# A build-time list scheduler for the order of all engine work, smaller last gating groups, 16 output slots and an input ring of 16, in a scan with a mixture of adapters

## The chip, the cores and the metric

The kernel runs on one core of one Trainium2 chip. The metric is the device time of one execution in microseconds (us), of which the profiler's span (first to last instruction) is about 1.8 us less. Times are medians of several executions. "ns" is written where nanoseconds are meant. PE is the matrix engine (TensorE), DVE is VectorE, ACT is ScalarE, POOL is GpSimd, SP is the engine whose queue issues the loads and stores.

## The reference, cut to what matters

A linear recurrence over 8 sequences of 6400 steps with 128 channels, then a top-2-of-8 mixture of rank-16 adapters on each of the 51200 rows, added to the row.

```python
def _attn_ref(a, b):                      # a, b: (8, 6400, 128) float32
    for t in range(S):
        h = a[:, t] * h + b[:, t]
        out[:, t] = h
def _moe_ref(x, w_gate, A, B):            # x = out as (51200, 128)
    logits = x @ w_gate                   # 8 experts
    topk = np.argpartition(-logits, K, axis=1)[:, :K]      # K = 2
    ... w = softmax of the two chosen logits ...
    delta[mask] += w[mask, k, None] * (x[mask] @ A[e]) @ B[e]
    return (x + delta).astype(np.float32)
```

## The kernel before

The rows are cut into 100 units of 512. For each unit w, PE transposes a and b into PSUM, the on-chip memory for its results (`pA`, `pB`), ACT copies `pA` to SBUF, the on-chip memory for everything else (`a_st`), DVE scans along time into `xT`. PE then makes the logits (`pL`) and x·A (`pZ`); once per group of 4 units the gates are made: an ACT copy, a DVE reduction, three POOL instructions, a second reduction, four POOL instructions, and a sigmoid on ACT. DVE multiplies `pZ` by the gates (`zw`), PE transposes the product (`pT`), ACT copies it (`zwT`), PE adds zwT·B and x in `pO`, ACT copies that to an output buffer (`outt`), and SP stores it.

In this program every engine runs a fixed list of instructions in order; semaphores make it wait for others. The list comes from a loop over steps written by hand:

```python
RING, XR, G, OU, NOUT = 24, 16, 4, 2, 4   # input units, x units, group, units per store, output buffers
LAG = G + 4
for s in range(-1, NU + LAG + 3):
    v = s - LAG
    if ok(v):      z_mm(v)                                  # PE
    if ok(s + 1):  transposes("A", s + 1); a_evac(s + 1)    # PE, ACT
    if ok(v - 1):  zw_tr(v - 1); t_evac(v - 1)              # PE, ACT
    if ok(s + 1):  transposes("B", s + 1)                   # PE
    if ok(v - 2):  delta(v - 2); o_evac(v - 2); ...store of a pair...
    if ok(s - 1):  logits(s - 1); ...l_evac at a group's end...
    if ok(s):      scan(s)                                  # DVE
    c = s - G - 1
    if c >= 0 and c % G == 0 and c // G < NU // G:
        gate_m1(c // G); gate1(c // G)                      # DVE, POOL
    c = s - G - 2
    if c >= 0 and c % G == 0 and c // G < NU // G:
        gate_m2(c // G); gate2(c // G)                      # DVE, POOL
        gate_sig(c // G)                                    # ACT: the sigmoid, in this same step
    if ok(v):      z_mul(v)                                 # DVE
    ...next load, when its ring slot comes free...
```

(Reformatted to one line per branch, cuts marked by dots.) There is one `pA`, one `pT`, one `pO`, two `pB`, two `pZ` and one `pL`, eight PSUM buffers in all.

## Time and profile before

| | before |
|---|---|
| time, median of 3 | 245.56 us |
| span of the profiled run | 243.7 us |
| first scan, last scan start | 6.6 us, 221.1 us |
| middle: period of 4 units | 8.46 us |
| from the start of the last scan to the end | 22.6 us |

No engine is full on average. From the page of before, the busy time of each engine, then two rows of its 40 slices of 6.1 us (each digit is the busy share in tenths):

```profile
PE 208.9 (86%) x2800; PEld 195.4 (80%) x2800; DVE 193.4 (79%) x257; ACT 172.5 (71%) x352; POOL 87.9 (36%) x181
...
DVE  0755988946889888988998898889889888987430
...
DMA  7999999999999999999999999999998233422444
```

DVE holds 8 or 9 tenths in the middle but falls at the start, near 50 us (the 4) and at the end, while DMA is busy until about 180 us and then at 2 to 4 tenths. So the kernel is read stage by stage.

**The middle.** The timeline of before on DVE in one period; columns are start, duration, instruction, and in brackets the idle time before it and what ended it:

```profile
91.53 0.68 DVE L412 TENSOR_TENSOR zw<-pZ,g 128x512 f16<-128x512 f32 x1
92.12 1.27 DVE L267 TENSOR_TENSOR_SCAN xT<-a_st,xT,pB 128x512 f16<-128x512 f32 x1
93.41 0.28 DVE L347 TENSOR_REDUCE m_0<-L_0 128x16 f32<-128x128 f32 x1
...
95.39 0.67 DVE L412 TENSOR_TENSOR zw<-pZ,g 128x512 f16<-128x512 f32 x1
96.84 1.28 DVE L267 TENSOR_TENSOR_SCAN xT<-a_st,xT,pB 128x512 f16<-128x512 f32 x1 [0.78 <-ACT a_st L249]
```

DVE starts one instruction right behind the other (a scan every 1.19 us, a multiply 0.59) until it waits 0.78 us for the `a_st` copy. The timeline of before on ACT at that time says why the copy was late:

```profile
94.08 0.59 ACT L454 COPY outt<-pO 128x512 f32<-128x512 f32 x1
96.02 0.31 ACT L390 ACTIVATE g<-um 128x128 f32<-128x128 f32 x1 [1.36 <-POOL um L379]
96.24 0.57 ACT L249 COPY a_st<-pA 128x512 f32<-128x512 f32 x1
```

ACT stands 1.36 us at the sigmoid, waiting for POOL; the copy behind it needs nothing from the sigmoid. This recurs in each group.

**The whole run.** The groups of waits of before (waiting instruction, what released it: us in total, times, longest):

```profile
ACT g L390 <- POOL um L379: 34.8, 24, 2.6
DVE xT L267 <- ACT a_st L249: 21.2, 23, 2.8
...
ACT outt L454 <- DMA out_dram<-outt: 6.0, 2, 3.5
```

The last line is the hole near 50 us: ACT waits twice, 3.5 and 2.5 us, for one of the 4 output buffers.

### The profile page before, as it was taken

The page shows a single profiled execution, that of the slowest core. Times are in us where ns is not written, and L with a number is a line of the kernel's source. Part 1 is how long each engine was busy: PE and PEld are TensorE (multiplying, and loading weights), DVE is VectorE, ACT ScalarE, POOL GpSimd, SP SyncE. Part 2 cuts the span into 40 slices and gives each one's busy share as a digit, 9 for nine tenths or more (in the row PEclk, how much of TensorE's full clock was granted, in tenths as well). Part 3 has the DMA queues.
Part 4 walks back from the last instruction along what each step waited for, and adds up shares of the span by engine and source line. Part 5 has one row for each costly group of instructions (what it writes and reads, how often), then busy time and mean ns, then how long its engine had stood idle before and what let it go on. Part 6 is the DMA issues. An engine that isn't in the chain of part 4 may idle for free.

```text
span 243.7 us, 6924 instructions
## 1 busy us (share of the span) xinstructions
PE 208.9 (86%) x2800; PEld 195.4 (80%) x2800; DVE 193.4 (79%) x257; ACT 172.5 (71%) x352; POOL 87.9 (36%) x181
## 2 busy tenths in 40 slices
PE   3766989867899999999999999999999999997592
PEld 2666888867889888988998898889889888986471
DVE  0755988946889888988998898889889888987430
ACT  3223587556777977887797788779777977977572
POOL 1005424503245235424522542353255235324500
PEclk9989999979999999999999999999999999999978
DMA  7999999999999999999999999999998233422444
GB/s 200 387 387 389 383 387 386 387 392 396 402 396 399 392 400 401 395 400 396 400 395 391 360 386 386 343 405 350 342 404 330 104 134 128 156 108 105 156 175 172
DMA packets 41424, 79.23 MB, mean 325 GB/s; under 512 B 2864, under 2 KB 2992, under 8 KB 41392
## 3 DMA queue, kind: packets, MB, share of 16 engines
q1 hardware_dynamic: 40064, 78.65, 86.7%
q8 instruction: 22, 0.36, 0.6%
q10 hardware_dynamic: 1328, 0.14, 0.4%
q14 instruction: 10, 0.08, 0.1%
HBM read 52.56 MB, written 26.21 MB: 323 GB/s over the span
## 4 chain that ended last, share of the span: by engine, by line
PE 32%; POOL 21%; DVE 20%; DMA 10%; ACT 8%; issue 6%; SPq 1%; POOLq 0%; DVEq 0%; ACTq 0%
DVE xT L267 12%; PE pA L237 10%; PE pB L237 8%; POOL pn L365 6%; DMA out_dram<-outt 5%; ACT a_st L249 5%; PE pT L421 5%; DVE zw L412 5%; DMA b_in<-in_b_dram 4%; POOL um L379 4%; PE pO L440 3%; PE pO L443 3%; PE pZ L398 2%; POOL d_0 L372 2%; POOL d_1 L372 2%
## 5 line engine op out<-in xcount | busy, mean ns | idle before, releaser
L267 DVE TENSOR_TENSOR_SCAN xT<-a_st,xT,pB 128x512 f16<-128x512 f32 x96 | 120.2, 1252 | 26.8 <-ACT a_st L249 21.2
L237 PE MATMUL pA<-ident_f,a_in 128*128 128x128 f32 x400 | 64.7, 286 | 18.5 <-ACT a_st L249 13.6
L249 ACT COPY a_st<-pA 128x512 f32<-128x512 f32 x100 | 58.8, 588 | 19.4 <-PE pA L237 18.4
L412 DVE TENSOR_TENSOR zw<-pZ,g 128x512 f16<-128x512 f32 x100 | 67.4, 675 | 5.1 <-PE pZ L398 3.2
L454 ACT COPY outt<-pO 128x512 f32<-128x512 f32 x100 | 58.9, 589 | 9.9 <-DMA out_dram<-outt 6.0
L237 PE MATMUL pB<-ident_f,b_in 128*128 128x128 f32 x400 | 62.8, 281 | 2.3 <-DMA b_in<-in_b_dram 2.3
L237 PEld LDWEIGHTS pA<-ident_f,a_in 128*128 128x128 f32 x400 | 43.8, 145 | 22.9 <-ACT a_st L249 16.8
L440 PE MATMUL pO<-cst_h,zwT 128*128 128x128 f16 x400 | 56.6, 222 | 5.6 <-ACT outt L454 5.5
L431 ACT COPY zwT<-pT 128x512 f16<-128x512 f16 x100 | 59.6, 596 | 1.0 <-PE pT L421 0.8
L443 PE MATMUL pO<-ident_h,xT 128*128 128x128 f16 x400 | 56.6, 222 | 0.0
L237 PEld LDWEIGHTS pB<-ident_f,b_in 128*128 128x128 f32 x400 | 44.0, 145 | 3.4 <-DMA b_in<-in_b_dram 3.2
L443 PEld LDWEIGHTS pO<-ident_h,xT 128*128 128x128 f16 x400 | 45.2, 115 | 1.0
L440 PEld LDWEIGHTS pO<-cst_h,zwT 128*128 128x128 f16 x400 | 39.4, 99 | 7.4 <-ACT outt L454 7.3
L421 PE MATMUL pT<-ident_h,zw 128*128 128x128 f16 x400 | 39.3, 222 | 4.3 <-ACT zwT L431 2.7
L398 PE MATMUL pZ<-cst_h,xT 128*128 128x128 f16 x400 | 39.7, 222 | 0.0
L421 PEld LDWEIGHTS pT<-ident_h,zw 128*128 128x128 f16 x400 | 28.8, 99 | 9.2 <-DVE zw L412 3.7
L390 ACT ACTIVATE g<-um 128x128 f32<-128x128 f32 x25 | 7.8, 311 | 34.8 <-POOL um L379 34.8
L323 POOL TENSOR_TENSOR d_0<-Lg,m_0 128x128 f32<-128x128 f32 x13 | 5.3, 408 | 71.5 <-DVE m_0 L312 71.5
L289 PE MATMUL pL<-cst_h,xT 128*128 128x8 f16 x400 | 27.1, 173 | 0.0
L398 PEld LDWEIGHTS pZ<-cst_h,xT 128*128 128x128 f16 x400 | 27.0, 116 | 0.0
L289 PEld LDWEIGHTS pL<-cst_h,xT 128*128 128x128 f16 x400 | 24.4, 116 | 0.1
L323 POOL TENSOR_TENSOR d_1<-Lg,m_1 128x128 f32<-128x128 f32 x12 | 4.9, 407 | 49.8 <-DVE m_1 L312 49.8
(29 smaller groups left out, 107.9 us busy)
## 6 DMA issues: line engine op xcount, KB each, us to landing
out_dram<-outt SPq DMA_DIRECT2D x50, 512.0 KB, 7.8
a_in<-in_a_dram SPq DMA_DIRECT2D x24, 1024.0 KB, 10.6
b_in<-in_b_dram SPq DMA_DIRECT2D x24, 1024.0 KB, 12.7
a_in<-in_a_dram SPq DMA_DIRECT2D x2, 256.0 KB, 3.6
b_in<-in_b_dram SPq DMA_DIRECT2D x2, 256.0 KB, 4.1
a_in<-in_a_dram SPq DMA_DIRECT2D x1, 512.0 KB, 5.5
b_in<-in_b_dram SPq DMA_DIRECT2D x1, 512.0 KB, 6.4
cst_f<-in_moe_A_dram ACTq DMA_DIRECT2D x1, 64.0 KB, 4.1
```

The source lines that it names most:

```text
L237: last = h.transpose(view[:, i, :], ring[:, w % RING, i * 128 : (i + 1) * 128], ident_f[:, :],)
L249: lambda h: h.copy(a_st[w % 2][:, :], pA[:, :]),
L267: last = h.tensor_tensor_scan(out=xT[:, x0 + lo : x0 + hi], data0=a_st[w % 2][:, lo:hi], data1=pB[w % 2][:, lo:hi], initial=init, op0=ALU. ...
L289: last = h.matmul(pL[:, c : c + E], x_block(w, i), wg_h)
L365: lambda h: h.tensor_scalar(pn[s][:, :, :], d2[s][:, :, :], 0.0, -1.0e30, ALU.is_lt, ALU.mult),
L398: last = h.matmul(pZ[w % 2][:, i * 128 : (i + 1) * 128], x_block(w, i), Acat_h)
L412: lambda h: h.tensor_tensor(out=oview, in0=zview, in1=gview, op=ALU.mult),
L421: last = h.transpose(pT[:, i * 128 : (i + 1) * 128], zw[w % 2][:, i, :], ident_h[:, :])
L431: lambda h: h.copy(zwT[w % 2][:, :], pT[:, 0:UT]),
L440: h.matmul(o, zwT[w % 2][:, i * 128 : (i + 1) * 128], Bcat_h, start=True, stop=False)
L443: last = h.matmul(o, x_block(w, i), ident_h[:, :], start=False, stop=True)
L454: lambda h: h.copy(outt[j % NOUT][:, w % OU, :], pO[:, :]),
```

## The change

The hand-written loop goes. Each instruction group gets a name, an engine, a priority key (its unit number plus an offset), an assumed duration and its dependencies; a list scheduler simulates the five engines and a 390 GB/s DMA link at build time and picks, on each engine as it falls free, the ready item with the lowest key. The result is again one fixed order for each engine. Beside that: gating groups of 4 end in groups of 2, 1, 1; loads are 1, 1 and then 2 units (before 1, 1, 2, then 4); 16 output slots instead of 4 pairs, the last two units stored singly; the input ring is 16 units instead of 24. The diff, cut to its core (assumed durations in ns):

```diff
+    def schedule(self, dma_rate):
+        ...
+            pick = min((x for x in cand[e] if x[0] <= t), key=lambda x: (x[1].key, x[0]))
+            self.order[e].append(op)
+            free[e] = t + op.busy
-    RING = 24
+    RING = 16
-    NOUT = 4
+    NOUT = 16
+    loads = cut((1, 1), 2, ())
+    groups = cut((), 4, (2, 1, 1))
+    stores = cut((), 2, (1, 1))
+            add(f"{kind}{w}", "pe", w - (0.3 if kind == "A" else 0), 440.0, ...)
+                f"scan{w}", "dve", w, 1140.0, emit, ...
+            add(f"Z{w}", "pe", w + 5, 230.0, emit, [f"scan{w}", f"mul{w - NZ}", "cst"])
+                f"mul{w}", "dve", w + 5.5, 600.0, ...
+            add(f"T{w}", "pe", w + 6, 225.0, emit, [f"mul{w}", f"tev{w - 1}", "idh"])
+                f"tev{w}", "act", w + 6, 480.0, ...      # needs T{w}, R{w - 2}
+            add(f"R{w}", "pe", w + 6.5, 455.0, emit, [f"tev{w}", f"oev{w - NO}"])
+                f"oev{w}", "act", w + 6.5, 480.0, ...    # needs R{w}, the slot's store
-        for s in range(-1, NU + LAG + 3):
-            ... the whole loop by hand ...
+        plan.schedule(390.0)
```

(Lines of several calls are joined here.) In what follows T is the transpose of the product into `pT`, "tev" its copy to `zwT`, R the output matmuls into `pO`, "oev" their copy to `outt`, as the change names them.

## The prediction

> **What bounds it now.** The span is 243.7 us (the time is about 1.9 us longer). No engine is full on average (page, part 1: PE 86%, DVE 79%, ACT 71%), so I read stages.
>
> - Middle (59 to 222 us). The chain of waits repeats every 8.46 us per 4 units (2.116 per unit). In one period (DVE timeline, 88.3 to 96.8 us) VectorE works back to back except for one gap of 0.78 us, charged to the a_st copy. That copy is late because ScalarE is stuck for 1.36 us at the sigmoid, which waits for POOL. The Trainium skill ("TensorE: Matmul & The Clock Gate", section "Architectural detail") calls ACT and DVE strict FIFO; the trace agrees: a copy that needs nothing from the sigmoid waits behind it. Outside that gap VectorE needs 7.68 us per 4 units (scan 1.19 start to start, multiply 0.59, reductions 0.19 each), 1.92 per unit; PE is also back to back there, 1.91 per unit.
> - Start (6.6 to 59 us). Only 23 scans. VectorE waits for pB behind 1 MB loads (2.7 us once); ScalarE waits twice for an output buffer (3.5 and 2.5 us, "ACT outt <- DMA"): only 4 store pairs exist, and stores queue behind loads (one took 13 us).
> - End. 22.6 us from the start of the last scan: fixed lag of 8 units, a full group's gating exposed, 512 KB last store.
> - DMA is busy until about 180 us, then 35 to 50%. It moves 78.65 MB; its best stretches show 397 to 402 GB/s, so about 198 us: near, but not binding in the middle.
>
> **What the change does.** Instruction kinds, sizes and bytes stay (a few small gating instructions are added). Order moves: (1) in the built program the sigmoid stands two units after the second reduction, about 3.8 us, while POOL's four instructions need about 2.0 us; the 0.78 us gap should go: 0.17 to 0.19 per unit. (2) Loads of 512 KB: first ten scans end near 20 us, not 25. (3) 16 output slots: the two output waits go, about 6 us of VectorE idle. (4) Last groups of 2, 1, 1, lag down to 5 to 6, single-unit last stores: tail about 16 us, saving 6.
>
> **Sum (an estimate from the durations above).** Ten scans by 20 us. Left for VectorE: 90 x 1.19 + 100 x 0.585 + 48 x 0.19 = 175 us; at 97% packed, 180: ends at 200. Exposed last gating 2 us, then transpose, copy, PE, copy, store of the last unit about 7 (7.6 in before): span 209 to 212. Nearly all of it is on the critical path, but PE (191 us plus a slow start), VectorE and DMA all end near 205 to 210, so a static order cannot make every stall vanish; I add 2 us. The shorter ring should not hurt: 16 units are 31 us, far over the 8 to 13 us from issue to landing.
>
> **Predicted: 214 us, 8 in 10 between 208 and 223.** Faster by over 2%: 0.97; within: 0.02; slower: 0.01.
>
> **What would show it.** Middle period 7.7 to 7.9 us per 4 units, DVE busy about 97%; "DVE xT <- ACT a_st" from 21 us to under 6; "ACT g <- POOL um" (34.8 us) below 8; "ACT outt <- DMA out_dram" gone; DMA busy to nearly the end, mean near 370 GB/s; tail about 16 us; instruction durations unchanged.
>
> **What would make it wrong.** DMA binding: below 385 GB/s with mixed traffic, waits on a_in/b_in would appear mid-run. The order was made with assumed durations (scan 1.14 against 1.19); if it mismatches, PE or ScalarE waits appear every unit and the period stays above 8 us. SP may hold loads behind an unready store. A lower granted clock would stretch everything.

## The result, and the profile after

222.91 us (222.17 to 223.05, 4 runs) against 245.55 us (4 runs): the ratio is 0.907, 95% interval 0.905 to 0.909. Ratios are computed as the mean time of one kernel's runs over that of the other's of the same rounds, so they are not quite the ratios of the medians quoted. The change saved 22.6 us; the prediction had said 214 us with a range of 208 to 223, so the result lies at the very edge of it.

| | before | after |
|---|---|---|
| span of the profiled run | 243.7 | 221.2 us |
| last scan starts | 221.1 | 197.35 us |
| middle: period of 4 units | 8.46 | 7.81 us |
| last scan start to end | 22.6 | 23.9 us |

The page after:

```profile
PE 204.4 (92%) x2800; PEld 195.6 (88%) x2800; DVE 191.5 (87%) x261; ACT 174.2 (79%) x356; POOL 90.5 (41%) x195
...
DVE  0499999999999999999999999999999999994320
...
DMA  7999999999999999999999999999999999843434
```

The holes at the start and near 50 us are gone; DVE is full until about 199 us, DMA until about 188. The chain that ended last is now PE's, 82% of the span (before, 32%). The waits after:

```profile
ACT outt L505 <- PE pO L494: 27.5, 76, 1.1
...
DVE zw L465 <- ACT g L442: 5.1, 21, 0.5
...
ACT g L442 <- POOL um L433: 0.5, 2, 0.3
```

The sigmoid waits 0.5 us instead of 34.8, and no wait of `outt` for a store is listed. In the timeline of after on DVE one period of the middle runs from one small gap to the next, 106.81 to 114.62, 7.81 us:

```profile
106.81 0.69 DVE L465 TENSOR_TENSOR zw<-pZ,g 128x512 f16<-128x512 f32 x1 [0.30 <-ACT g L442]
107.42 0.28 DVE L369 TENSOR_REDUCE m_0<-Lg 128x16 f32<-128x128 f32 x1
...
113.11 1.27 DVE L313 TENSOR_TENSOR_SCAN xT<-a_st,xT,pB 128x512 f16<-128x512 f32 x1
114.62 0.69 DVE L465 TENSOR_TENSOR zw<-pZ,g 128x512 f16<-128x512 f32 x1 [0.23 <-ACT g L442]
```

What did not shrink is the tail: 23.9 us from the start of the last scan, 1.3 us more than before. Nine multiplies and eleven sets of output matmuls are left when the last scan starts or soon after, and they go at 1.8 to 1.9 us each (the last one 2.2), although no engine is busy for much over half of the time there. The window of after from 200 us (us: busy time with instructions of PE, PEld, DVE, ACT, POOL, then granted clock, DMA share and GB/s):

```profile
200.00:221.00 21.00, 10.94 (x144) 9.01 (x144) 6.12 (x13) 11.20 (x26) 5.61 (x20) 0.82 0.40 151
```

The timelines of after in the tail, PE first:

```profile
207.26 0.41 PE L449 MATMUL pZ<-cst_h,xT 128*128 128x128 f16 x4 [0.79 <-DVE zw L465]
207.51 0.22 PE L493 MATMUL pO<-cst_h,zwT 128*128 128x128 f16 x1
...
207.95 0.39 PE L472 MATMUL pT<-ident_h,zw 128*128 128x128 f16 x4
209.13 0.41 PE L449 MATMUL pZ<-cst_h,xT 128*128 128x128 f16 x4 [0.79 <-DVE zw L465]
209.38 0.22 PE L493 MATMUL pO<-cst_h,zwT 128*128 128x128 f16 x1
```

then ACT, and last DVE:

```profile
206.77 0.59 ACT L483 COPY zwT<-pT 128x512 f16<-128x512 f16 x1
...
208.15 0.59 ACT L505 COPY outt<-pO 128x512 f32<-128x512 f32 x1 [0.67 <-PE pO L494]
208.64 0.59 ACT L483 COPY zwT<-pT 128x512 f16<-128x512 f16 x1
210.03 0.59 ACT L505 COPY outt<-pO 128x512 f32<-128x512 f32 x1 [0.80 <-PE pO L494]
```

```profile
206.51 0.69 DVE L465 TENSOR_TENSOR zw<-pZ,g 128x512 f16<-128x512 f32 x1 [1.18 <-PE pT L472]
...
208.38 0.69 DVE L465 TENSOR_TENSOR zw<-pZ,g 128x512 f16<-128x512 f32 x1 [1.09 <-PE pT L472]
```

Two loops can be followed there. R of one unit (207.51) lets the output copy start (208.15); the `zwT` copy of the next unit stands behind that copy on ACT (208.64 to 209.23), and the next R needs it (209.38): 1.87 us. Likewise on PE: a transpose that needs only an older product and the `zwT` copy of 206.77 to 207.36 stands in PE's order behind a Z that waits for the newest multiply (207.26) and behind R, and so starts at 207.95; the next multiply waits for it. The Trainium skill ("TensorE: Matmul & The Clock Gate", Part 2, step-by-step) says that matmuls stay in program order and only weight loads are pulled ahead; the trace agrees, the order of PE's matmuls is that of the list.

### The profile page after: what moved, and what is told of

It reads as the page before. It is cut to its first block, busy times and chain, and to the rows that moved or that the text cites. A ratio compares the mean times of both kernels' runs of the same rounds, so it can differ in the third digit from the quotient of the medians.

```text
span 221.2 us, 6969 instructions
## 1 busy us (share of the span) xinstructions
PE 204.4 (92%) x2800; PEld 195.6 (88%) x2800; DVE 191.5 (87%) x261; ACT 174.2 (79%) x356; POOL 90.5 (41%) x195
## 3 DMA queue, kind: packets, MB, share of 16 engines
q1 hardware_dynamic: 40848, 78.65, 94.3%
## 4 chain that ended last, share of the span: by engine, by line
PE 82%; DVE 7%; ACT 3%; DMA 2%; issue 2%; POOL 1%; SPq 1%; DVEq 0%; ACTq 0%; POOLq 0%
PE pA L282 19%; PE pB L282 18%; PE pZ L449 12%; PE pO L493 10%; PE pO L494 10%; PE pT L472 9%; DVE xT L313 5%; PE pL L338 5%; DMA b_in<-in_b_dram 2%; DVE zw L465 2%; ACT outt L505 2%; ACT zwT L483 1%; SPq L266 1%; POOL pn L417 0%; ACT a_st L296 0%
## 5 line engine op out<-in xcount | busy, mean ns | idle before, releaser
L282 PE MATMUL pA<-ident_f,a_in 128*128 128x128 f32 x400 | 63.1, 281 | 3.8 <-DMA a_in<-in_a_dram 3.8
L282 PE MATMUL pB<-ident_f,b_in 128*128 128x128 f32 x400 | 61.2, 277 | 0.1
L483 ACT COPY zwT<-pT 128x512 f16<-128x512 f16 x100 | 58.9, 589 | 0.4 <-PE pT L472 0.4
L282 PEld LDWEIGHTS pA<-ident_f,a_in 128*128 128x128 f32 x400 | 43.0, 143 | 5.3 <-DMA a_in<-in_a_dram 4.2
L282 PEld LDWEIGHTS pB<-ident_f,b_in 128*128 128x128 f32 x400 | 46.9, 142 | 0.9 <-DMA b_in<-in_b_dram 0.9
L449 PE MATMUL pZ<-cst_h,xT 128*128 128x128 f16 x400 | 40.7, 225 | 3.6 <-DVE zw L465 3.5
L472 PEld LDWEIGHTS pT<-ident_h,zw 128*128 128x128 f16 x400 | 26.7, 98 | 0.0
L338 PEld LDWEIGHTS pL<-cst_h,xT 128*128 128x128 f16 x400 | 23.5, 117 | 3.6 <-DVE xT L313 3.4
L377 POOL TENSOR_TENSOR d_0<-Lg,m_0 128x128 f32<-128x128 f32 (+2 forms) x14 | 5.4, 388 | 36.2 <-DVE m_0 L369 36.2
L409 POOL TENSOR_TENSOR d_0<-Lg,m_0 128x128 f32<-128x128 f32 (+2 forms) x14 | 5.5, 390 | 25.7 <-DVE m_0 L401 25.7
L409 POOL TENSOR_TENSOR d_1<-Lg,m_1 128x128 f32<-128x128 f32 (+1 forms) x13 | 5.2, 397 | 23.7 <-DVE m_1 L401 23.2
```

What stands on the lines that cost most here:

```text
L282: last = h.transpose(view[:, i, :], ring[:, w % RING, i * 128 : (i + 1) * 128], ident_f[:, :])
L338: last = h.matmul(pL[:, c : c + E], x_block(w, i), wg_h)
L409: lambda h: h.tensor_tensor(out=v(d2[s]), in0=v(Lg[s]), in1=bc(m2[s]), op=ALU.subtract),
L449: last = h.matmul(pZ[w % NZ][:, i * 128 : (i + 1) * 128], x_block(w, i), Acat_h)
L472: last = h.transpose(pT[:, i * 128 : (i + 1) * 128], zw[w % 2][:, i, :], ident_h[:, :])
L483: lambda h: h.copy(zwT[w % 2][:, :], pT[:, 0:UT]),
```

## The experiments

Theories for the result. **(A)** The gain of the middle comes from taking the sigmoid out of the way of the `a_st` copy, and that of the start from the output slots; the list scheduler as such is not needed. Rival: its packing is what counts. **(B)** The tail is paced by the loops that its fixed order closes. Rivals: exposed gating, or the granted TensorE clock, which is 0.82 on average after 200 us. **(C)** In the middle PE is the limit. Rival: DVE.

Twelve kernels ran, all gave correct results, each with 4 timed executions beside the kernel before on the same chip (medians of before 244.65 to 245.49 us). They ran in three sets on three chips and the change was not run again beside them, while before itself differs by up to 0.8 us between the sets; differences of that size from set to set are not read below.

| kernel | median us | ratio to before (95%) |
|---|---|---|
| the change | 222.91 | 0.907 (0.905 to 0.909) |
| before, sigmoid one step later | 233.11 | 0.952 (0.950 to 0.954) |
| before, 16 output slots | 240.06 | 0.980 (0.977 to 0.983) |
| before, both | 218.52 | 0.892 (0.890 to 0.894) |
| change, tail order swapped | 218.18 | 0.890 (0.887 to 0.893) |
| change, tail swapped, second pO | 216.78 | 0.884 (0.882 to 0.886) |
| change, all groups of 4 | 222.39 | 0.907 (0.905 to 0.909) |
| change, first logits held back | 222.85 | 0.911 (0.906 to 0.917) |
| change, logits twice | 231.46 | 0.944 (0.942 to 0.947) |
| change, 8 output slots (3 runs) | 231.19 | 0.943 (0.939 to 0.947) |
| change, ring of 24 | 223.07 | 0.912 (0.908 to 0.916) |
| before, both, and start and tail | 216.58 | 0.884 (0.881 to 0.886) |
| the same, small last groups | 217.78 | 0.890 (0.886 to 0.893) |

### The sigmoid alone

```diff
                 gate2(c // G)
+            c = s - G - 3
+            if c >= 0 and c % G == 0 and c // G < NU // G:
                 gate_sig(c // G)
```

> The kernel before with one edit: the sigmoid is issued one step later, nothing else. Theory (the 0.78 us gap per four units is ScalarE stuck at the sigmoid): the period falls from 8.46 to 7.7 to 7.9 us, ACT g <- POOL um from 34.8 us to a few; about 20 groups x 0.6 to 0.75 gives 12 to 15 us, time 231 to 234, if no other wait replaces it; the start, the output-buffer waits and the tail stay. Rival (the period is set elsewhere, by PE or DMA, and the gap would reappear at another wait): under 4 us gained.

233.11 us, as the theory expected. Where nothing else interferes the period is 7.9 us (first reductions at 88.84 and 96.74 us). But the total hides a second effect. The waits of this kernel:

```profile
ACT outt L454 <- DMA out_dram<-outt: 14.1, 7, 6.7
```

The wait for output buffers grew from 6.0 to 14.1 us: units are now finished faster than four buffers can be written out, and a store takes a median of 11.4 us from issue to landing, 7.8 in before. Part of the gain was handed to a new wait.

### The output slots alone

```diff
-    NOUT = 4
+    NOUT = 8        # pairs: 16 slots
```

> The kernel before with 8 output pairs (16 slots) instead of 4, nothing else. Theory (stores stand behind loads at the start and ScalarE waits for a buffer, 3.5 and 2.5 us): ACT outt <- DMA vanishes, the middle and the tail stay, time 239 to 241. Rival (the wait only moves, for instance into later loads, since DMA is full until 180 us): 244 to 246.

240.06 us, clearly faster than before, though whether by over 2% is open (0.977 to 0.983): the wait for stores is gone, the period is still 8.46 us (scans after the gap start at 91.92 and 100.38 us) and the sigmoid still waits 36.0 us in total.

### Both edits in the hand-written order

> Both edits together in the kernel before: sigmoid later and 16 output slots, hand-written order kept. If the two gains add: 226 to 229 us, which would leave 3 to 6 us for everything else the change did (scheduler, small loads, small groups). If the list scheduler's packing is what matters: 232 or more.

218.52 us, far below the expectation and 4.4 us below the whole change. The gains more than add: alone 11.7 and 4.7 us, together 26.3 (each from the 244.77 us of before in those rounds). Each edit had run into what the other removes. In the timeline of this kernel on DVE one period takes 7.58 us, from 88.04 to 95.62, with no gap in it, less than the scheduler's 7.81 (13 of the 17 periods between 55 and 190 us take 7.58 to 7.67, the mean of all is 7.69):

```profile
88.04 0.29 DVE L347 TENSOR_REDUCE m<-L 128x16 f32<-128x128 f32 x1
...
95.62 0.29 DVE L347 TENSOR_REDUCE m<-L 128x16 f32<-128x128 f32 x1
```

Its last scan starts at 196.75 us, 0.6 us before that of the change, although its start is slower, and its tail takes 19.55 us. So theory A holds and its rival falls: in the hand-written order the two edits are enough for the whole gain, and the packing is not needed. (The change also has smaller loads and another order at its start; what each edit is worth inside it was tested only for the slots, next.)

### 8 output slots in the changed kernel

```diff
-    NOUT = 16
+    NOUT = 8
```

> The changed kernel with 8 output slots (4 pairs, as before) instead of 16, the list scheduler kept. Theory (a faster middle asks for its output buffers sooner; a store takes about 11 us from issue to landing, so 8 slots of 1.95 us are too few): ACT outt <- DMA out_dram returns with 5 us or more in total, time 227 to 233. Rival (the scheduler orders around it, the 16 slots are only for comfort): 222 to 224.

231.19 us, inside the theory's range; the slots are worth 8.3 us here too. (One of its four executions was slow and is left out.) But the form was not as expected: the wait of `outt` for a store is only 1.6 us in total. The scheduler knows the slots, and has changed the order on all engines; in the stretch of 60 to 90 us DVE is busy 25.19 of 30 us, with many short waits. Which of these carry the loss was not separated. The loss also hides a gain: the last scan starts at 210.58 us, 13.2 us later than in the change, and the tail after it takes 18.0 us instead of 23.9.

### Ring of 24 in the changed kernel

```diff
-    RING = 16
+    RING = 24
```

> The changed kernel with an input ring of 24 units instead of 16. Theory (16 units of 1.95 us far exceed the 11 us from issue to landing, so the ring is not what limits): 222 to 224, same waits. Rival (the shorter ring is a part of the gain, since fewer loads stand before the first store): 2 us or more slower.

223.07 us, the same as the change: in total the length of the ring is not a part of the gain, and shortening it cost nothing. But "same waits" was missed. The scheduler, given another ring, made another order: in the profiled run (224.59 us) the last scan starts at 202.20 us, 4.9 later, and the tail takes 20.6 us, 3.3 less. Such an edit changes the whole schedule, not one thing.

### The order of the tail

Only the last ten units, after the scheduler has run:

```diff
+        for j in range(89, 99):
+            move(pe, f"T{j + 1}", f"R{j}")      # before R{j}, and before a Z just ahead of it
+            move(act, f"tev{j + 1}", f"oev{j}")
```

> The changed kernel with only the order of its last ten units altered: on PE the transpose of unit j+1 goes before the output matmuls of unit j, on ScalarE the zwT copy of unit j+1 before the output copy of unit j. Theory (serial loop of the static order): in the changed kernel the tail runs at 1.8 to 1.9 us per unit because the loop output matmuls 0.44, latency 0.2, output copy 0.48, zwT copy 0.6, latency 0.15 closes on itself; with the swap the zwT copy leaves the loop, so about 1.3 us per unit, last scan to end 23.9 -> 18 to 19 us, time 222.9 -> 217 to 218. Rival A (the tail is long because the last small gating groups are exposed one after another): the swap changes under 1 us. Rival B (the granted TensorE clock, 0.82 after 200 us): also under 1 us.

218.18 us, against 222.91, with the same instructions and the same gating groups: rival A falls, and from the start of the last scan to the end it is 18.9 us instead of 23.9. Rival B falls too: in the change the matmuls still take 0.22 us up to 213 us, when the loop has long run at 1.87, only the last two units are slowed (0.31 us); and one of its executions had a mean clock of 0.997 and took 223.05 us, another 0.981 and 222.86. The timeline of this kernel on ACT shows a unit every 1.3 us, with the `zwT` copy ahead of the output copy, which now waits 0.22 us for PE:

```profile
210.41 0.59 ACT L521 COPY outt<-pO 128x512 f32<-128x512 f32 x1
210.90 0.59 ACT L499 COPY zwT<-pT 128x512 f16<-128x512 f16 x1
211.71 0.59 ACT L521 COPY outt<-pO 128x512 f32<-128x512 f32 x1 [0.22 <-PE pO L510]
```

The 1.3 us that remain are R, its output copy and the next R, on the single `pO`.

The swap moves entries on PE and on ACT at once; which of the two loops held the pace was not separated. And it restores what the old loop had: there `zw_tr(v - 1); t_evac(v - 1)` stand before `delta(v - 2); o_evac(v - 2)`. The keys of the change (R at w + 6.5, T of the next unit at w + 7, and the same for their copies) turned this around.

### A second output buffer in the tail

With the swap, and for the last ten units in turn (`pA` is free once the last a has been copied):

```diff
+        W2 = NU - 10
+        def o_ps(w):
+            return pA if w >= W2 and (w - W2) % 2 == 0 else pO[w % NO]
```

> As the tail swap, and the last ten units alternate their output between pO and pA, which is free once the last a_st copy is done. Theory: with two buffers the next output matmuls no longer wait for the output copy; ScalarE's two copies (0.96 to 1.0 us per unit) set the pace, last scan to end 15 to 16 us, time 214 to 216. Rivals A and B: no more than 1 us below the changed kernel, 222.

216.78 us, 1.4 us below the swap, but not the 214 to 216 expected. The tail takes 17.7 us; units come every 1.2 us, not every 1.0, and the last multiply waits 0.79 us for the last sigmoid.

### Groups of 4 to the end

```diff
-    groups = cut((), 4, (2, 1, 1))
+    groups = cut((), 4, ())
```

> The changed kernel without the small last gating groups (25 groups of 4). Theory (the tail is paced by the loop of output matmuls and copies, and gating hides behind it): costs only the delay of the first unit of the last group, time 223 to 226, last scan to end 24 to 27 us. Rival A (exposed gating dominates the tail, and small groups are what keeps it short): 227 or more. A result at or below 222.9 says that the small groups bought nothing.

222.39 us: the small last groups bought nothing in the changed kernel. This is the other half of the test of B: a change of the last gating moves nothing, a change of the tail's order moves 4.7 us.

### First logits held back

```diff
-            add(f"L{w}", ..., [f"scan{w}", f"lev{k - 1}", "cst"])
+            add(f"L{w}", ..., [f"scan{w}", f"lev{k - 1}", "cst"] + ([f"B{w + 2}"] if w < 4 else []))
-            add(f"Z{w}", ..., [f"scan{w}", f"mul{w - NZ}", "cst"])
+            add(f"Z{w}", ..., [f"scan{w}", f"mul{w - NZ}", "cst"] + ([f"B{w + 4}"] if w < 2 else []))
```

> The changed kernel with the first logits and Z matmuls held back behind the transposes of the units two and four later, so that PE's fixed order does not make the third unit's transposes wait for the second scan. Theory (head-of-line wait in the fixed order at the start, 0.86 and 1.57 us of VectorE idle before the second and third scan): the tenth scan starts near 19.5 instead of 21.1 us and the end comes 1 to 2 us earlier, about 221. Rival (the start is set by when the loads land and by the slow PE clock): no change, within 0.5 us.

222.85 us, no gain; the expectation missed. The tenth scan starts at 20.59 us, only 0.5 us earlier, and by other changes in the schedule the last scan even starts 2.4 us earlier, at 194.93; the tail then takes 25.2 us. Scans that are ahead do not help while the units behind them go through the slow loop.

### Logits twice

```diff
+                    h.matmul(pL[:, c : c + E], x_block(w, i), wg_h)
                     last = h.matmul(pL[:, c : c + E], x_block(w, i), wg_h)
```

> The changed kernel with each logits matmul issued twice (same result), 0.13 us more PE work per unit. Theory (PE is the limit of the middle, 100% busy there): the period of four units grows from 7.81 by about 0.5 us to 8.3, time 222.9 -> 233 to 235. Rival (VectorE is the limit, with 0.23 us to spare in 7.81): the period grows by 0.3 us or less, time under 231.

231.46 us, between the two. The timeline of this kernel on DVE:

```profile
102.98 0.28 DVE L370 TENSOR_REDUCE m<-Lg 128x16 f32<-128x128 f32 x1
...
111.18 0.28 DVE L370 TENSOR_REDUCE m<-Lg 128x16 f32<-128x128 f32 x1
```

The period grew from 7.81 to 8.20 us, by 0.39 and not by the 0.52 of added PE work (4 x 0.13). PE's own work was 4 x 1.91 = 7.64 us before the addition and 8.16 with it (an estimate from the back-to-back stretches of the kernel before, good to about 0.1: the hand order ran the same matmuls in 7.58). So the middle was within about 0.2 us of PE's limit, and this experiment put it there; DVE, busy 29.1 of 30 us in the change, is just as near. DMA is a third candidate: 7.81 us per 4 units ask for 403 GB/s (3.146 MB), and 398 to 399 were moved from 60 to 180 us, though no wait of the change names a load or a store there. C is settled only so far: all three are close, and the hand order's 7.58 shows that 7.81 is not a floor.

### The two edits, with start and tail

Sigmoid later, 16 slots, loads of 1, 1 and then 2 units, the second `pO` in the tail, the last two units stored singly:

```diff
-    for n in (1, 1, 2):
+    for n in (1, 1):
-        n = min(4, NU - u)
+        n = min(2, NU - u)
+            return pA if w >= W2 and (w - W2) % 2 == 0 else pO
+                if v - 2 >= NU - OU:
+                    store_one(v - 2)
```

> The hand-ordered kernel of before with the sigmoid one step later and 16 output slots (218.5 us measured), plus loads of two units, the last ten units' outputs alternating between pO and pA, and the last pair stored one unit at a time. Theory: two-unit loads give about 2 us at the start, the second output buffer and the short last store 2 to 3 us at the end, time 213 to 215. Rival (hand order already hides these): 217 to 219.

216.58 us, the lowest median, but not to be told from the change with swapped tail and second `pO` (216.78); the expectation, 213 to 215, was missed. The tail gave 1.5 us, 18.1 instead of 19.55, where 2 to 3 were expected. The start gave 2.6 us (the two half scans of unit 12 at 27.27 and 27.93 instead of 29.89 and 30.54), and yet the last scan starts at 196.74 us, as in the kernel with two edits (196.75). Where the gain was given back, the windows tell; first the kernel with the two edits, then this one (us: busy time with instructions of PE, PEld, DVE, ACT, POOL, then granted clock, DMA share and GB/s):

```profile
120.00:150.00 30.00, 30.00 (x442) 29.64 (x441) 29.97 (x42) 27.51 (x56) 13.48 (x28) 1.00 1.05 398
150.00:180.00 30.00, 30.00 (x442) 29.64 (x440) 29.64 (x40) 27.17 (x56) 13.27 (x27) 1.00 1.05 399
```

```profile
120.00:150.00 30.00, 29.86 (x430) 28.48 (x429) 29.00 (x40) 24.78 (x54) 13.57 (x28) 1.00 1.05 399
150.00:180.00 30.00, 29.54 (x419) 27.51 (x417) 28.28 (x38) 24.11 (x55) 12.13 (x25) 1.00 1.05 399
```

DVE loses 2.3 us (57.3 busy instead of 59.6) between 120 and 180 us: a period takes 7.6 us at first and 8.1 from about 130 us on (the kernel with two edits slows to 8.0 only from about 172). Its waits:

```profile
ACT outt L460 <- PE pA L238: 7.5, 9, 0.9
...
ACT outt L460 <- DMA out_dram<-outt: 3.2, 5, 0.8
```

The first line looks like stores too. The one looked at, at 157.08 us, comes 0.86 us after the last matmul into its `pO` ended, at 156.22, and two units after a copy that the trace does put down to a store (153.05); only every second unit, the first of a pair, must wait for a buffer. So even 16 slots run short here. DMA is full in both kernels. At 7.58 us per 4 units the kernel asks for 3.146 MB in 7.58 us, 415 GB/s (78.65 MB for 100 units); the runs show 397 to 400 in stretches of 30 us and 406 in the best single slice of a page. So DMA is probably the next limit; no run here took bytes away to show it.

### The same with small last groups

The last groups 2, 1, 1 instead of 4, in the hand-written order (`groups`, and each gating step keyed to a group's last unit).

> As the previous run, and the last gating groups are 2, 1, 1 units. Theory (in the hand order the last group's gating is exposed, 1.2 and 1.55 us of VectorE idle in the tail, since nothing slower stands beside it): 1 to 2 us less than the previous run, about 212. Rival (as with groups of 4 in the changed kernel, small groups buy nothing): within 0.5 us of the previous run.

217.78 us, 1.2 us slower than without. Small last groups paid in neither order.

## Why the prediction was right or wrong

- **The middle: right.** The predicted period was 7.7 to 7.9 us, 7.81 came. The cause was right too: moving the sigmoid alone, in the old order, does it, and the wait for POOL went from 34.8 to 0.5 us. "DVE busy about 97%" came as 29.0 to 29.3 of 30 us.
- **The output waits: right, and larger than costed.** About 6 us were predicted for 16 slots. Alone they gave 4.7; but in a kernel with the faster middle they are worth far more, 14.6 us (233.11 to 218.52), because the need for buffers grows with the pace. The prediction costed each part in the old kernel's surroundings.
- **The start: 2.3 us too good.** "First ten scans end near 20 us": they ended near 22.3. The experiment that held the first logits back did not recover it.
- **The tail: the step that failed.** The prediction said "lag down to 5 to 6 ... tail about 16 us, saving 6", and in the sum it charged the last multiplies at DVE's speed, 0.585 us each, plus "exposed last gating 2 us". The tail took 23.9 us. First, the offsets of 5.5 in the keys are not the lag: in the middle the first multiply of a group comes after the scan eight units ahead of it (the multiply at 114.62 us in the timeline of after is that of unit 48, the scan at 113.11 that of unit 56), and nine multiplies stood behind the last scan, as the built order had shown. Second, those units went at 1.87 us each, not 0.6, round a loop of four engines' fixed orders. The swap of two pairs of entries shows it: 1.3 us per unit, 5.0 us off the tail.
- **Sum.** The last scan was predicted to start near 193.8 us (20, plus 175.0 for the 175 us of work less nine multiplies, packed at 97%, minus 1.2 for the scan itself) and started at 197.35: 2.3 us from the start, about 1.2 from the middle. With 7.9 us of tail, less the 2 us that the prediction had added for stalls, that is 9.4 us, close to the 9.2 between the predicted span (about 212) and the measured 221.2. The prediction was right in direction, and for the middle and the output waits in mechanism. The tail is the term that failed, 16 for 23.9 us: its lag did not fall, and its pace was that of a loop. That the total still fell inside the range, by 0.1 us, is luck.
- **The ring: right.** 24 instead of 16 changes nothing.
- **DMA: nearly.** "Mean near 370 GB/s" was 358, full to about 188 us; no wait of the change shows it as the limit, and it may be the limit below 217 us.

## What to carry to other kernels

Where engines run fixed orders, look first for the one instruction that waits longest at the head of an in-order queue and move it by one step: here two edits of a few lines gave more than a rewritten schedule. A greedy scheduler that ranks by key sees no loops; in the tail, where no engine is full, follow who waits for whom until the loop closes, and cost the last units at that loop's time. Test parts together as well as alone: a part that removes a wait is worth little while another wait stands behind it.

## What the Trainium skill lacked or had wrong

- "TensorE: Matmul & The Clock Gate" states that ACT and DVE are strict FIFO and that matmuls keep program order, and the traces agree (a copy 1.36 us behind a sigmoid; 0.79 us behind a Z). No page that I read says what follows for a static order: that two in-order engines can close a loop that no data dependency demands, here 1.87 us per unit instead of 1.3.
- "DMA: Bandwidth & Descriptors" (section Bandwidth) says in a note that for transfers between HBM and SBUF the HBM side, about 358 GB/s, binds, as if a core alone were held to it; higher up, beside a table of single-core figures, the same section gives that rate to a core whose neighbour streams too. With one core running, mixed loads and stores held 398 to 399 GB/s here in each stretch of 30 us from 60 to 180 us. "Perfetto Trace Analysis" (section Engine Utilization, Roofline) has it right for a single core: above the 358 share, below about 435.
- The same DMA page gives about 2.0 us plus bytes over 436 GB/s for one DMA (fitted on the other issue path). A 256 KB store at the end, with little else queued, landed in 2.0 us (the formula gives an estimate of 2.6), but with the queue full a 512 KB transfer took 11 us from issue to landing. The page has no rule for that wait in the queue, and it bears on the size of an output ring: in the change 8 slots were too few and 16 left no such wait, in the fastest kernel 16 still left 3.2 us of it.
